# Attention and two MoE layers in one kernel: the q and k loads, the reciprocal of the softmax sums and its small DMAs are moved in the step table

## Chip, cores and metric

The kernel runs on one core of one Trainium2 chip. The metric is the device time of one execution in microseconds (us). Times of engines are counted from the start of the span of one profiled execution.

## The reference

```python
# attention: q, k, v are (4, 8, 1152, 64), float32
q_pool = q.reshape(B, H, S // 2, 2, D).mean(axis=3)
scores = scale * np.matmul(q_pool, k.transpose(0, 1, 3, 2))
scores = scores - np.max(scores, axis=-1, keepdims=True)
attn = np.exp(scores)
attn = attn / (np.sum(attn, axis=-1, keepdims=True) + 1e-09)
attn = np.matmul(attn, v)
# first MoE layer: x is (2304, 512), weights arrive as 64 bit floats
h = np.maximum(x @ w_in, 0.0)
x = h * h @ w_out
# second MoE layer: 8 experts, each token to one expert, at most N // 8 tokens each,
# by a sort of all logits x @ w_gate; then relu(x[mask] @ w1[e]) @ w2[e]
```

## The kernel before

The program has three stretches. For about 790 us it works on the 32 heads of the attention (`Attention.run`), and between the heads it already makes the first MoE layer's hidden rows; then that layer's second product and the routing follow, then the eight experts. The change touches only the first stretch.

**Steps.** A head has 18 steps (`STEPS`, L118). The table `AT` (L45 to L47) gives each part of the work of head n a step, counted from 18n: `lq` and `lk` load q and k, `qs` adds pairs of q rows on POOL (`q_sum`, L187), `kh0` to `kl` split k into two parts (L171 on ACT, L178 on POOL), `kt` and `qt` transpose them on PE and copy them out of PSUM (L221 to L249, copies by DVE or ACT), `pk` are fifteen products whose row maxima DVE takes (L263, L265). The scores of a head (`score`, L278, L279) and their exponentials (L282 on ACT) run one per step, four steps ahead. In the last step of a head `av` makes P times V (L307) and the row sums (L313 or L319). `run` calls `av`, then a score, then whatever has been put off to this step with `at`, then the table's entries, in that order; this is the order of instructions in each engine's queue. Each engine takes its queue in order, and SP, which issues the DMAs, does too: a DMA that waits holds back all that stand behind it.

**The sums' way.** `av` copies the row sums to `row` (L324 on ACT) and moves them with small DMAs into `rc`, 96 partitions by 6 (L329; the heads 0 to 10 have two partial sums per query and so four DMAs, the heads from 11 on, `ADD_HEADS`, have two, because there POOL adds the P tiles up beforehand, `ss`, L292). Five steps later (`recip`) POOL adds the two parts (L335, heads 0 to 10) and the constant 1e-9 (L336), and DVE takes the reciprocal (L337). One step on (`spread`) a DMA writes it to `rs_scr` in DRAM (L340) and another reads it back as 64 rows into `rb` (L341). From step 13 (`norm`) of the odd heads POOL multiplies y by `rb` in three pieces (L483).

**What stands between.** Up to about 291 us one part of the first MoE layer's weights per four steps is read as 64 bit words and turned into float32 by DVE and ACT (`F64.load`: `words` L87, `size` L90 and L96, `sign` L93 and L99, `value` L105). A part of `w_in` is split on ACT (`wih`, L433) and POOL (`wil`, L437); a part of `w_out` is transposed (L453) and stored in DRAM (`wos`, L447). When the eight heads of a batch are done, `batch_h` inserts the products of the first MoE layer (L510) between the steps of the next heads, half a batch at a time; a half takes about four heads, and starts with four `split_x`, whose rest `xl` (L493) POOL makes. Before step 216 (`ORDER_FROM`) these inserted parts run behind a step's other work, from there on ahead of it. The sums of the gate (`ls`, L533 to L538) come from DVE and leave by SP.

**Buffers.** q and k share two `raw` tiles, so a load waits until POOL or ACT has read the tile of two loads before. `value` has two tiles too.

```python
AT = dict(lq=-49, qs=-43, lk=-47, ..., recip=5, spread=6, norm=13,
          high=0, wlow=4, turn=3, gate=5, ...)
```

Of the kernel before, what the change touches and what calls it, by code (L numbers as in the profile page):

```python
# [14 lines left out]
AF = mybir.ActivationFunctionType  # L15
OP = mybir.AluOpType
# [7 lines left out]
HQ = NQ // 2  # L24
# [9 lines left out]
EPS = 1e-9  # L34
# [7 lines left out]
SC, HB, XB = 3, 2, 3  # L42
PEAK_H = 8
PB, WB = 11, 3
AT = dict(lq=-49, qs=-43, lk=-47, qh0=-41, qh1=-41, ql=-38, kh0=-39, kh1=-37, kl=-36, kt0=-28, kt1=-28, kt2=-25,  # L45
          qt0=-25, t2=-22, pk=-23, lv=-12, qt1=-6, qt2=-6, recip=5, spread=6, norm=13,
          high=0, wlow=4, turn=3, gate=5, f0=9, f1=9, f2=9, f3=11, f4=11, f5=14)  # L47
TL, TA = 1, 5
ITERS = 5
START, FIRST, FAST, SLOW, LAST = 36, 32, 8, 16, 14  # L50
# [20 lines left out]
class F64:  # L71
# [7 lines left out]
    def load(self, src, then):  # L79
# [29 lines left out]
        for d, f in enumerate((shift, sign, merge, unit, size, join)):  # L109
            self.at(AT[f"f{d}"], f)  # L110


class Attention:
# [172 lines left out]
    def total(self, n, c, hf):  # L286

        d = self.st[n]
        if c == 1 and hf == 0:
            d["ss"] = self.w1.tile([128, 2, HQ], F32, name="ss")  # L290
        s = d["ss"][:, hf]
        self.nc.gpsimd.tensor_tensor(s, d["P", 0][:, hf] if c == 1 else s, d["P", c][:, hf], op=OP.add)  # L292

    def av(self, n):
        nc = self.nc
        odd = n % 2
        d = self.st[n]
        mine = slice(64, 128) if odd else slice(0, 64)
        pr = n // 2
        if odd == 0:  # L300
            self.y[pr] = self.yp.tile([128, NQ], F32, name="y")
            self.rb[pr] = self.w1.tile([128, NQ], F32, name="rb")
        y, rb = self.y[pr], self.rb[pr]
        A = self.px.tile([128, 512], F32, name="wx")
        for c in range(9):
            for hf in range(2):
                nc.tensor.matmul(A[hf * 64:(hf + 1) * 64, :HQ], d["vf"][:, c], d["P", c][:, hf],  # L307
                                 start=(c == 0), stop=(c == 8))
        t = self.px.tile([128, 512], F32, name="wx")
        if n >= ADD_HEADS:  # L310
            parts = 1
            for hf in range(2):
                nc.tensor.matmul(t[hf * 64:(hf + 1) * 64, :HQ], self.one, d["ss"][:, hf], start=True, stop=True)  # L313
        else:
            parts = 2
            for c in range(9):
                for hf in range(2):
                    r = hf * 64 + c % 2 * 32
                    nc.tensor.matmul(t[r:r + 32, :HQ], self.one[:, 0:32], d["P", c][:, hf],  # L319
                                     start=(c < 2), stop=(c > 6))  # L320
        for hf in range(2):
            nc.scalar.activation(y[mine, hf * HQ:(hf + 1) * HQ], A[hf * 64:(hf + 1) * 64, :HQ], AF.Copy)
        row = self.w1.tile([128, HQ], F32, name="row")
        nc.scalar.activation(row, t[:, :HQ], AF.Copy)  # L324
        rc = self.w2.tile([96, 2, 6], F32, name="rc")
        for hf in range(2):
            for j in range(parts):
                r = hf * 64 + j * 32
                nc.sync.dma_start(rc[hf * 48:(hf + 1) * 48, j, :], row[r:r + 1])  # L329
        for c in range(9):  # L330
            del d["P", c]

        def recip():
            if parts == 2:
                nc.gpsimd.tensor_tensor(rc[:, 0], rc[:, 0], rc[:, 1], op=OP.add)  # L335
            nc.gpsimd.tensor_scalar(rc[:, 0], rc[:, 0], EPS, None, op0=OP.add)  # L336
            nc.vector.reciprocal(rc[:, 0], rc[:, 0])  # L337

        def spread():
            nc.sync.dma_start(self.scratch[n:n + 1, :], rc[:, 0])  # L340
            nc.sync.dma_start(rb[mine, :], bass.AP(tensor=self.scratch.tensor,  # L341
                                                   offset=self.scratch.offset + n * NQ,
                                                   ap=[[0, 64], [1, NQ]]))

        self.at(AT["recip"], recip)
        self.at(AT["spread"], spread)
        if odd:
            for k, f in self.emit(pr, y, rb):
                self.at(k, f)
            del self.y[pr], self.rb[pr]  # L350
# [4 lines left out]
    def events(self, n):  # L355
# [8 lines left out]
        for name, (f, *a) in todo.items():  # L364
            ev.setdefault(AT["lq" if n == 0 and name == "lk" else name], []).append((f, n, *a))
        if n < 2:
            ev.setdefault(AT["kt0"] - 1, []).append((self.fill, n))
        for i in range(15):
            ev.setdefault(AT["pk"] + i, []).append((self.peak, n, i))
        return ev  # L370
# [28 lines left out]
def fused_kernel(ctx, tc, q, k, v, w_in, w_out, w_gate, w1, w2, out, dbg=None, upto=9):  # L399
    nc = tc.nc  # L400
# [6 lines left out]
    wos = dram("wo_scr", (FF, DM))  # L407
# [16 lines left out]
    def setup(f64, raw):  # L424

        gt = raw.tile([128, 4, E], F32, name="gt")
        nc.sync.dma_start(gt, w_gate.rearrange("(c p) e -> p c e", p=128))
        TT = {}

        def w_in_part(c, sl):  # L430
            def then(a):
                def high():
                    nc.scalar.activation(wih[:, c, sl], a, AF.Copy)  # L433

                def low(i):
                    sh = slice(sl.start + i * 128, sl.start + i * 128 + 128)
                    nc.gpsimd.tensor_tensor(wil[:, c, sh], a[:, i * 128:i * 128 + 128], wih[:, c, sh].bitcast(F32),  # L437
                                            op=OP.subtract)

                return [(AT["high"], high)] + [(AT["wlow"] + i, lambda i=i: low(i)) for i in range(2)]  # L440

            f64.load(wiv[c * 128:(c + 1) * 128, sl, :], then)

        def w_out_part(f, j):
            def then(a):
                def turn():
                    nc.sync.dma_start(wos[f * 128:(f + 1) * 128, j * 256:(j + 1) * 256], a)  # L447
                    if j == 0:
                        TT[f] = raw.tile([128, 4, 128], F32, name="wo_t", bufs=1)
                    tt = TT[f]  # L450
                    p = px.tile([128, 512], F32, name="wx")
                    for c in range(2):
                        nc.tensor.transpose(p[:, c * 128:(c + 1) * 128], a[:, c * 128:(c + 1) * 128], cm.idf)  # L453
                    nc.scalar.activation(tt[:, 2 * j:2 * j + 2, :], p[:, :256], AF.Copy)

                def gate():
                    tt = TT.pop(f)
                    g = px.tile([128, 512], F32, name="wx")
                    for c in range(4):
                        nc.tensor.matmul(g[:, :E], tt[:, c, :], gt[:, c, :], start=(c == 0), stop=(c == 3))  # L460

                    def split():
                        nc.vector.tensor_copy(Wg[:, f, 0:E], g[:, :E])

                    f64.at(1, split)

                return [(AT["turn"], turn)] + ([(AT["gate"], gate)] if j else [])

            f64.load(wov[f * 128:(f + 1) * 128, j * 256:(j + 1) * 256, :], then)

        for f in range(0, NF, 2):
            for i in range(4):
                w_in_part(i, slice(f * 128, f * 128 + 256))
                yield
                w_out_part(f + i // 2, i % 2)
                yield
# [130 lines left out]
    with ExitStack() as ea:  # L607
# [4 lines left out]
        parts, taken = setup(f64, raw), 0  # L612
# [581 lines left out]
```

## Time and profile before

| what | us |
|---|---|
| median of three runs | 1339.25 |
| the three runs | 1338.96, 1339.25, 1346.77 |
| the profiled execution | 1348.34 |
| its span | 1346.5 |
| PE busy | 1255.8 (93%) |
| DVE busy | 709.6 (53%) |
| ACT busy | 705.6 (52%) |
| POOL busy | 667.8 (50%) |

PE is TensorE, DVE VectorE, ACT ScalarE, POOL GpSimd, SP the engine that issues the DMAs. The span runs from the first to the last instruction of the one profiled execution; 1.84 us of that execution lie around it. In a row of the timeline the first number is the start, the second the duration of the row, and what stands in brackets is how long the engine was idle before and what released it. A row of the waits gives the total, how often, and the longest.

### The profile page before, as it was taken

The page shows a single profiled execution, that of the slowest core. Times are in us where ns is not written, and L with a number is a line of the kernel's source. Part 1 is how long each engine was busy: PE and PEld are TensorE (multiplying, and loading weights), DVE is VectorE, ACT ScalarE, POOL GpSimd, SP SyncE. Part 2 cuts the span into 40 slices and gives each one's busy share as a digit, 9 for nine tenths or more (in the row PEclk, how much of TensorE's full clock was granted, in tenths as well). Part 3 has the DMA queues.
Part 4 walks back from the last instruction along what each step waited for, and adds up shares of the span by engine and source line. Part 5 has one row for each costly group of instructions (what it writes and reads, how often), then busy time and mean ns, then how long its engine had stood idle before and what let it go on. Part 6 is the DMA issues. An engine that isn't in the chain of part 4 may idle for free. (4 is left out here: it accounts for less than half of the span.)

```text
span 1346.5 us, 25250 instructions
## 1 busy us (share of the span) xinstructions
PE 1255.8 (93%) x9033; PEld 1057.1 (79%) x9033; DVE 709.6 (53%) x1654; ACT 705.6 (52%) x1816; POOL 667.8 (50%) x962
## 2 busy tenths in 40 slices
PE   6897887999899899998999999999999979999997
PEld 4665665688788788887887889777777759999997
DVE  8767466466545354444454201168777724665552
ACT  6767476577566566566665646222222214445441
POOL 5333133248777787868777724266655301221111
PEclk9999899899999999999998999899999988999999
DMA  6435235234324232323322135534344314555541
GB/s 179 144 99 154 86 99 158 80 118 129 88 72 112 63 100 83 85 81 84 91 81 77 46 114 181 150 110 125 119 132 150 107 45 139 191 200 192 184 141 36
DMA packets 136388, 155.60 MB, mean 116 GB/s; under 512 B 19168, under 2 KB 97248, under 8 KB 136256
## 3 DMA queue, kind: packets, MB, share of 16 engines
q1 hardware_dynamic: 133040, 144.21, 35.6%
q0 software_dynamic: 3072, 9.44, 2.3%
q8 instruction: 73, 1.20, 0.4%
q14 instruction: 59, 0.48, 0.1%
q10 hardware_dynamic: 144, 0.26, 0.1%
HBM read 111.46 MB, written 32.87 MB: 107 GB/s over the span
## 5 line engine op out<-in xcount | busy, mean ns | idle before, releaser
L265 DVE TENSOR_REDUCE mx<-wx 128x1 f32<-128x384 f32 (+1 forms) x424 | 227.2, 549 | 240.7 <-PE wx L263 238.7
L282 ACT ACTIVATE P<-sc 128x288 f32<-128x288 f32 x576 | 226.1, 411 | 96.3 <-PE sc L279 89.3
L292 POOL TENSOR_TENSOR ss<-ss,P 128x288 f32<-128x288 f32 x294 | 231.1, 811 | 11.6 <-ACT P L282 9.1
L278 PE MATMUL sc<-M,T 128*128 128x288 f32 x576 | 179.9, 313 | 1.6 <-ACT P L282 1.6
L279 PE MATMUL sc<-M,t 128*128 128x288 f32 x576 | 173.4, 301 | 3.8 <-DVE M L246 3.7
L263 PE MATMUL wx<-T,M 128*128 128x384 f32 (+1 forms) x424 | 151.6, 358 | 21.5 <-DVE mx L265 17.4
L933 POOL TENSOR_TENSOR hl<-h,hh 128x256 fp32r<-128x256 f32 x130 | 101.6, 803 | 108.9 <-ACT hh L931 106.0
L307 PE MATMUL wx<-P,vf 128*64 128x288 f32 x1152 | 152.3, 420 | 0.8 <-DVE mx L265 0.8
L510 PE MATMUL h<-xh,wih 128*128 128x288 f32 x448 | 141.8, 316 | 0.0
L510 PE MATMUL h<-xh,wil 128*128 128x288 f32 x448 | 134.2, 300 | 2.0 <-POOL wil L437 2.0
L510 PE MATMUL h<-xl,wih 128*128 128x288 f32 x448 | 133.8, 299 | 0.0
L307 PEld LDWEIGHTS wx<-P,vf 128*64 128x64 f32 x1152 | 82.1, 141 | 61.5 <-issue 6.7
L278 PEld LDWEIGHTS sc<-M,T 128*128 128x128 f32 x576 | 111.4, 193 | 19.6 <-issue 6.9
L956 PE MATMUL x2p<-woh,hh 128*128 128x512 f32 x288 | 118.0, 410 | 0.0
L956 PE MATMUL x2p<-woh,hl 128*128 128x512 f32 x288 | 117.5, 408 | 0.0
L956 PE MATMUL x2p<-wol,hh 128*128 128x512 f32 x288 | 117.0, 406 | 0.0
L931 ACT ACTIVATE hh<-h 128x512 fp32r<-128x512 f32 x72 | 45.3, 630 | 135.5 <-PE x2p L956 125.1
L279 PEld LDWEIGHTS sc<-M,t 128*128 128x128 f32 x576 | 111.3, 193 | 6.3 <-DVE M L246 5.9
L178 POOL TENSOR_TENSOR ks<-raw,ks 128x192 fp32r<-128x192 f32 x93 | 55.8, 622 | 90.3 <-ACT ks L171 90.3
L263 PEld LDWEIGHTS wx<-T,M 128*128 128x128 f32 (+1 forms) x424 | 77.4, 183 | 28.3 <-DVE mx L265 21.7
L510 PEld LDWEIGHTS h<-xh,wih 128*128 128x128 f32 x448 | 86.2, 192 | 10.3 <-issue 10.2
L1068 POOL DMA_INDIRECT xg<-x_scr,ix x24 | 27.1, 1129 | 130.5 <-PE ept L1081 88.6
(200 smaller groups left out, 2952.8 us busy)
## 6 DMA issues: line engine op xcount, KB each, us to landing
eraw<-in_moe_w_dram SPq DMA_DIRECT2D x56, 512.0 KB
h_scr<-h2st SPq DMA_DIRECT2D x64, 288.0 KB
h<-h_scr SPq DMA_DIRECT2D x72, 256.0 KB
raw<-in_k_dram SPq DMA_DIRECT2D x32, 288.0 KB
t<-T SPq DMA_DIRECT2D x32, 288.0 KB
vf<-in_v_dram SPq DMA_DIRECT2D x32, 288.0 KB
raw<-in_q_dram SPq DMA_DIRECT2D x32, 256.0 KB
words<-in_moe_w_in_dram SPq DMA_DIRECT2D x32, 256.0 KB
```

What stands on the lines that cost most here:

```text
L178: eng.tensor_tensor(ks[:, c, 0:64], d["kn"][:, c], ks[:, c, 64:128].bitcast(F32), op=OP.subtract)
L263: nc.tensor.matmul(t[:m, :384], d["M1"][:, c * 128:c * 128 + m], d["T1"][:, j * 384:(j + 1) * 384], start=True, stop=True)
L265: nc.vector.tensor_reduce(mx[:m, c, j:j + 1], t[:m, :384], axis=AX.X, op=OP.max)
L278: nc.tensor.matmul(t[:, :HQ], d["T1"][:, kk], d["M1"][:, qr], start=True, stop=False)
L279: nc.tensor.matmul(t[:, :HQ], d["T2"][:, kk], d["M2"][:, qr], start=False, stop=True)
L282: nc.scalar.activation(d["P", c][:, hf], t[:, :HQ], AF.Exp, scale=1.0 / (2.0 * math.sqrt(D)))
L292: self.nc.gpsimd.tensor_tensor(s, d["P", 0][:, hf] if c == 1 else s, d["P", c][:, hf], op=OP.add)
L307: nc.tensor.matmul(A[hf * 64:(hf + 1) * 64, :HQ], d["vf"][:, c], d["P", c][:, hf], start=(c == 0), stop=(c == 8))
L510: nc.tensor.matmul(p[:, :HQ], a[:, c, fs], x, start=(j == 0), stop=(j == 11))
L931: self.nc.scalar.activation(hh, t, AF.Copy)
L933: self.eng.tensor_tensor(hl[:, i:i + 2], t[:, i:i + 2], hh[:, i:i + 2].bitcast(F32), op=OP.subtract)
L956: nc.tensor.matmul(self.p, a[:, f, :], x[:, f0 + f, :], start=(f0 + f == 0 and i == 0), stop=(f0 + f == NF - 1 and i == 2))
```

## The change

The loads of q and k get earlier steps; the reciprocal is parted from the addition of the two sums (`total`) and, with its spreading, comes three steps later, the multiplication by it one step later; the constant 1e-9 goes into ACT's copy of the sums (half of it where there are two parts); one DMA now moves both halves of a sum, two instead of four in heads 0 to 10 and one instead of two in the others; the store of a `w_out` part gets a step of its own, one behind its transposes.

```diff
-AT = dict(lq=-49, qs=-43, lk=-47, qh0=-41, ...
-          qt0=-25, t2=-22, pk=-23, lv=-12, qt1=-6, qt2=-6, recip=5, spread=6, norm=13,
-          high=0, wlow=4, turn=3, gate=5, f0=9, f1=9, f2=9, f3=11, f4=11, f5=14)
+AT = dict(lq=-55, qs=-43, lk=-50, qh0=-41, ...
+          qt0=-25, t2=-22, pk=-23, lv=-12, qt1=-6, qt2=-6, total=5, recip=8, spread=9, norm=14,
+          high=0, wlow=4, turn=3, keep=4, gate=5, f0=9, f1=9, f2=9, f3=11, f4=11, f5=14)
...
-        nc.scalar.activation(row, t[:, :HQ], AF.Copy)
+        nc.scalar.activation(row, t[:, :HQ], AF.Copy, bias=EPS / parts)
         rc = self.w2.tile([96, 2, 6], F32, name="rc")
-        for hf in range(2):
-            for j in range(parts):
-                r = hf * 64 + j * 32
-                nc.sync.dma_start(rc[hf * 48:(hf + 1) * 48, j, :], row[r:r + 1])
+        for j in range(parts):
+            nc.sync.dma_start(rc[:, j, :], row[j * 32:j * 32 + 65:64])
...
-        def recip():
+        def total():
             if parts == 2:
                 nc.gpsimd.tensor_tensor(rc[:, 0], rc[:, 0], rc[:, 1], op=OP.add)
-            nc.gpsimd.tensor_scalar(rc[:, 0], rc[:, 0], EPS, None, op0=OP.add)
+
+        def recip():
             nc.vector.reciprocal(rc[:, 0], rc[:, 0])
...
+        self.at(AT["total"], total)
         self.at(AT["recip"], recip)
         self.at(AT["spread"], spread)
...
                 def turn():
-                    nc.sync.dma_start(wos[f * 128:(f + 1) * 128, j * 256:(j + 1) * 256], a)
...
+                def keep():
+                    nc.sync.dma_start(wos[f * 128:(f + 1) * 128, j * 256:(j + 1) * 256], a)
...
-                return [(AT["turn"], turn)] + ([(AT["gate"], gate)] if j else [])
+                return [(AT["turn"], turn), (AT["keep"], keep)] + ([(AT["gate"], gate)] if j else [])
```

The order of PE and ACT stays as it was. DVE keeps its instructions, POOL loses the 32 additions of the constant, SP 43 of the 86 small DMAs.

The queue of SP at the start, of before (the first loads, `gt` the gate's weights, `words` the first parts of the MoE weights):

```order
L159 DMA raw<-in_q_dram 128x4x128
L160 DMA raw<-in_q_dram 64x128
L153 DMA raw<-in_k_dram 128x576
L427 DMA gt<-in_moe_w_gate_dram 128x4x8
L87 DMA words<-in_moe_w_in_dram 128x512
L87 DMA words<-in_moe_w_out_dram 128x512
L159 DMA raw<-in_q_dram 128x4x128
L160 DMA raw<-in_q_dram 64x128
```

and of the changed kernel:

```order
L159 DMA raw<-in_q_dram 128x4x128
L160 DMA raw<-in_q_dram 64x128
L153 DMA raw<-in_k_dram 128x576
L159 DMA raw<-in_q_dram 128x4x128
L160 DMA raw<-in_q_dram 64x128
L427 DMA gt<-in_moe_w_gate_dram 128x4x8
L87 DMA words<-in_moe_w_in_dram 128x512
L87 DMA words<-in_moe_w_out_dram 128x512
```

The load of head 1's q has moved ahead of the gate's weights and of the first two parts of the MoE weights.

The queue of SP behind the end of head 3, of before (`rc` the sums of head 3, `rs_scr` and `rb` its reciprocal, `wo_scr` the store of a `w_out` part):

```order
L329 DMA rc<-row 48x1x6 x4
L87 DMA words<-in_moe_w_out_dram 128x512
L447 DMA wo_scr<-value 128x256
L87 DMA words<-in_moe_w_in_dram 128x512
L340 DMA rs_scr<-rc 96x6
L341 DMA rb<-rs_scr 64x576
L159 DMA raw<-in_q_dram 128x4x128
L160 DMA raw<-in_q_dram 64x128
```

and of the changed kernel, where L327, L339, L340 and L456 are the old L329, L340, L341 and L447:

```order
L327 DMA rc<-row 96x1x6 x2
L159 DMA raw<-in_q_dram 128x4x128
L160 DMA raw<-in_q_dram 64x128
L87 DMA words<-in_moe_w_out_dram 128x512
L456 DMA wo_scr<-value 128x256
L87 DMA words<-in_moe_w_in_dram 128x512
L153 DMA raw<-in_k_dram 128x576
L165 DMA vf_105<-in_v_dram 128x576
L87 DMA words<-in_moe_w_out_dram 128x512
L339 DMA rs_scr<-rc 96x6
L340 DMA rb<-rs_scr 64x576
```

The q load stood behind the two DMAs that wait for the reciprocal, and stands now right behind the sums' own; k has passed the two as well.

The queue of DVE in a later head, about 444 to 454 us of before (`mx` row maxima, `ls` a sum of the gate):

```order
L265 TENSOR_REDUCE mx<-wx 128x1 x7
L535 TENSOR_TENSOR ls<-wx,ls 128x288
L265 TENSOR_REDUCE mx<-wx 128x1 x2
L337 RECIPROCAL rc<-rc 96x6
L265 TENSOR_REDUCE mx<-wx 128x1 x3
L267 TENSOR_REDUCE q_0_109<-mx 128x4
L265 TENSOR_REDUCE mx<-wx 64x1 x3
```

and of the changed kernel, where L336 and L537 are the old L337 and L535:

```order
L265 TENSOR_REDUCE mx<-wx 128x1 x7
L537 TENSOR_TENSOR ls<-wx,ls 128x288
L265 TENSOR_REDUCE mx<-wx 128x1 x5
L267 TENSOR_REDUCE q_0_109<-mx 128x4
L336 RECIPROCAL rc<-rc 96x6
L265 TENSOR_REDUCE mx<-wx 64x1 x3
```

The reciprocal has moved behind three maxima and the reduction over them.

The queue of SP behind the last head, of before (`h_scr` hidden rows, `lg_scr` the gate's sums):

```order
L329 DMA rc<-row 48x1x6 x2
L522 DMA h_scr<-h2st 128x2x288 x2
L340 DMA rs_scr<-rc 96x6
L341 DMA rb<-rs_scr 64x576
L522 DMA h_scr<-h2st 128x2x288
L538 DMA lg_scr<-ls 8x288 x4
```

and of the changed kernel, with L524 and L540 for the old L522 and L538:

```order
L327 DMA rc<-row 96x1x6
L524 DMA h_scr<-h2st 128x2x288 x3
L540 DMA lg_scr<-ls 8x288 x4
L339 DMA rs_scr<-rc 96x6
L340 DMA rb<-rs_scr 64x576
```

The spreading of the last reciprocal has moved behind one more store of hidden rows and the four stores of the gate's sums.

## Rows read from the trace of the kernel before

**Rows 1.** The page, busy time of each engine: us, share of the span, instructions.
```profile
PE 1255.8 (93%) x9033; PEld 1057.1 (79%) x9033; DVE 709.6 (53%) x1654; ACT 705.6 (52%) x1816; POOL 667.8 (50%) x962
```
**Rows 2.** Waits of 0 to 300 us: who waited for whom, total, times, longest.
```profile
POOL qs L187 <- DMA raw<-in_q_dram: 45.5, 13, 6.7
...
DVE value L105 <- POOL wil L437: 9.5, 6, 2.7
```
**Rows 3.** Timeline of SP, POOL, DVE and PE, 121 to 135 us.
```profile
124.49 0.49 SPq L341 DMA_DIRECT2D rb<-rs_scr  x1
125.08 0.53 SPq L159 DMA_DIRECT2D raw<-in_q_dram  x1
...
128.37 1.28 POOL L187 TENSOR_TENSOR qs<-raw 128x256 f32<-128x256 f32 x2 [5.92 <-DMA raw<-in_q_dram]
...
132.18 1.76 DVE L105 TENSOR_TENSOR value<-sign,size 128x256 f32<-128x256 f32 x1 [2.65 <-POOL wil L437]
...
134.08 0.66 PE L453 MATMUL wx<-idf,value 128*128 128x128 f32 x2 [3.36 <-DVE value L105]
```
**Rows 4.** Windows: us, busy time of PE, PEld, DVE, ACT, POOL, granted clock, DMA.
```profile
130.00:135.00 5.00, 1.64 (x11) 1.11 (x9) 2.83 (x4) 3.14 (x10) 3.65 (x8) 0.67 0.91 237
135.00:140.00 5.00, 5.00 (x29) 2.69 (x30) 1.76 (x5) 0.16 (x1) 0.00 (x0) 0.65 0.09 27
```
**Rows 5.** The same view, the first 300 us.
```profile
0.00:300.00 300.00, 254.77 (x1878) 190.23 (x1879) 194.98 (x478) 197.89 (x587) 102.37 (x200) 0.95 0.43 125
```
**Rows 6.** Waits of 300 to 760 us.
```profile
DVE rc L337 <- POOL rc L336: 37.7, 19, 3.6
...
PE wx L263 <- DVE mx L265: 14.7, 5, 3.3
```
**Rows 7.** Timeline of POOL, DVE and PE, 449 to 459 us, and PE's next such stall.
```profile
449.95 0.79 POOL L493 TENSOR_TENSOR xl<-y,xh 128x288 fp32r<-128x288 f32 x1
450.82 0.23 POOL L336 TENSOR_SCALAR rc<-rc 96x6 f32<-96x6 f32 x1
...
454.91 0.81 POOL L493 TENSOR_TENSOR xl<-y,xh 128x288 fp32r<-128x288 f32 x1
...
451.76 0.39 PE L263 MATMUL wx<-T,M 128*64 128x384 f32 x1 [3.28 <-DVE mx L265]
...
457.98 0.29 PE L278 MATMUL sc<-M,T 128*128 128x288 f32 x1
...
542.80 0.39 PE L263 MATMUL wx<-T,M 128*64 128x384 f32 x1 [3.07 <-DVE mx L265]
```
**Rows 8.** Timeline of SP, ACT and PE at the start.
```profile
2.96 0.51 SPq L87 DMA_DIRECT2D words<-in_moe_w_in_dram  x1
...
4.64 0.38 SPq L159 DMA_DIRECT2D raw<-in_q_dram  x1
...
6.72 0.45 ACT L93 ACTIVATE sign<-words 128x256 f32<-128x256 f32 x1 [0.66 <-DMA words<-in_moe_w_in_dram]
...
9.67 0.69 PE L263 MATMUL wx<-T,M 128*128 128x384 f32 x1 [1.21 <-ACT M L207]
```
**Rows 9.** Timeline of SP, POOL and PE behind the last head.
```profile
787.56 0.34 SPq L340 DMA_DIRECT2D rs_scr<-rc  x1
...
791.54 1.30 SPq L538 DMA_DIRECT2D lg_scr<-ls  x4
...
792.62 1.71 POOL L483 TENSOR_TENSOR y<-y,rb 128x192 f32<-128x192 f32 x3 [8.38 <-issue]
...
796.66 0.29 PE L510 MATMUL wx<-xh,wih 128*128 128x288 f32 x1
```
**Rows 10.** The page, one DMA queue (packets, MB, share of 16 engines); timeline, sums of head 6.
```profile
q1 hardware_dynamic: 133040, 144.21, 35.6%
...
194.05 2.45 SPq L329 DMA_DIRECT2D rc<-row  x4
...
197.93 0.20 POOL L335 TENSOR_TENSOR rc<-rc 96x6 f32<-96x6 f32 x1 [1.92 <-DMA rc<-row]
```

More of the change, by code (lines that the diff above doesn't have):

```diff
@@ L44 @@
 PB, WB = 11, 3
-AT = dict(lq=-49, qs=-43, lk=-47, qh0=-41, qh1=-41, ql=-38, kh0=-39, kh1=-37, kl=-36, kt0=-28, kt1=-28, kt2=-25,
-          qt0=-25, t2=-22, pk=-23, lv=-12, qt1=-6, qt2=-6, recip=5, spread=6, norm=13,
-          high=0, wlow=4, turn=3, gate=5, f0=9, f1=9, f2=9, f3=11, f4=11, f5=14)
+AT = dict(lq=-55, qs=-43, lk=-50, qh0=-41, qh1=-41, ql=-38, kh0=-39, kh1=-37, kl=-36, kt0=-28, kt1=-28, kt2=-25,
+          qt0=-25, t2=-22, pk=-23, lv=-12, qt1=-6, qt2=-6, total=5, recip=8, spread=9, norm=14,
+          high=0, wlow=4, turn=3, keep=4, gate=5, f0=9, f1=9, f2=9, f3=11, f4=11, f5=14)
 TL, TA = 1, 5
```

## The prediction

> **What bounds the kernel now.** I read the page's busy times first. PE is busy for 93% of the span, every other engine for about half of it [rows 1], and PE's order is not changed, so the change can win or lose only where PE waits. I then listed PE's stalls of 1 us and more in the attention from its timeline, and asked the views of waits, by stretch, who stood in front of each.
>
> *Early, up to 300 us.* POOL waits 13 times, 45.5 us in all, for the q load before it can add q's pairs, and DVE waits 9.5 us for POOL's split of a weight [rows 2]. Behind the end of head 3 it reads as one chain [rows 3]: on SP the load of q stands behind the DMA that reads back the reciprocal, which itself can go only when the reciprocal is in DRAM (124.49). So q is issued at 125.08 and POOL starts on it at 128.37, after 5.92 us idle. The weights' splits stand behind it; DVE's `value` waits 2.65 us for one of them and then takes 1.76 us; PE waits 3.36 us for `value`. Of this kind are four PE stalls, at 63, 134, 157 and 235 us: 2.16, 3.36, 3.27 and 3.73, 12.5 us together; DVE's side of it is the 9.5 us of waits [rows 2] and what two long `value` take over their usual 0.41. The granted clock falls behind such a stall: 0.67 and 0.65 in the ten microseconds around this one [rows 4], where PE had stood still.
>
> *Late, from 300 us.* DVE waits for POOL's addition of 1e-9, 19 times and 37.7 us [rows 6], although the sums have long landed: POOL works off a queue of P additions. Most of it hides. Where a half batch starts it does not: `xl` at 449.95, the constant at 450.82, and behind the reciprocal the row maxima, so that PE stands 3.28 us until 451.76 [rows 7]. PE's waits for maxima are 14.7 us in five places [rows 6]: the five half starts from 361 to 726 us.
>
> **The change part by part.**
>
> *q and k loads.* Five DMAs no longer stand in front of q, the two that wait for the reciprocal among them: it is issued right behind the sums' own DMAs, six steps earlier. A step is 542.80 − 451.76 = 91.0 us [rows 7] over 72 steps, so 1.26 us; six are 7.6. Behind head 3 that is an issue at 125.08 − 7.6 = 117.5 instead of 125.08 and, with the 3.3 us that it took from there to POOL's start, a landing at 120.8, where POOL stood ready at 128.37 − 5.92 = 122.45 [rows 3]. With the wait the neighbour in time goes too: the 1.76 us of `value` lay beside POOL's late q work. Of the 12.5 us I take 10 off. The rest stays because at 63 and 157 us PE's next wait, for a copy that DVE makes behind `value`, is only about 1 us shorter than the stall. Bounds: 5 to 12.5. What the clock costs in the first 300 us is at most 300 × (1 − 0.95) = 15 us [rows 5]; the windows of 5 us around the four stalls hold 12 of these, about 10 outside the stalls themselves. I take 7 off, between 0 and 10, since some small stall may leave the clock low just as well.
>
> *Reciprocal apart from its addition, constant on ACT.* 32 additions of 0.23 us leave POOL [rows 7], and 43 DMA issues of 2.45 / 4 = 0.61 us leave SP [rows 10]. Neither engine sets the end, so that by itself is worth 0. The bias costs ACT no instruction; I put it at 0, between −0.4 and +1 us over the 32 copies. What counts is that the reciprocal no longer waits for POOL. The next bound at a half start is `xl`: the fourth one ends at 454.91 + 0.81 = 455.72 now, and 0.3 earlier without the constant, 455.4. PE's products behind it then go on at about 455.5, where they stood at 457.98 [rows 7]: 2.4 us for the whole place, stall and slow clock together. Five places at 2.0 to 2.8 give 12 off. Bounds: 2.5 (each `xl` stops PE in turn, and the clock stays low) and 19 (all 14.7 us and half as much clock).
>
> *The start.* Head 1's q now stands before the first MoE weights on SP, and it shares a `raw` tile that POOL must first have read: before, it went at 4.64, and the weights at 2.96 [rows 8]. Now the weights follow at about 6.1, 3.1 us later. ACT's `sign`, which waits for them and ran at 6.72, stands ahead of the copies that PE's first maxima product at 9.67 needs. ACT had 0.66 us idle there, so 1.9 to 3.1 us are lost: +2.5.
>
> *The end.* Behind the last head the DMA of the reciprocal went at 787.56. It now stands behind the four stores of the gate's sums, which end at 791.54 + 1.30 = 792.84 [rows 9], 5.3 us later. Read back faster than before (nothing stands between: 1.5 us instead of 1.84), the multiplication that began at 792.62 starts 3 us or more later, at 797.7 at the latest, takes 1.71, and ACT's and DVE's splits another 1.7. PE wanted the result at 796.66 and would get it at about 800: 3.4 us, and up to 1.7 us of clock. +4.5, between +2 and +6.
>
> *Small new waits.* DVE's next-but-one `value` now waits for the store one step later, and at three places `value` needs a split that stands behind `total`, with 0.2 to 0.5 us to spare. Five places at 0 to 1 us: +2.5.
>
> *The merged DMA.* Head 6's four DMAs began at 194.05, the issue of the last ended at 196.50, and POOL added at 197.93 [rows 10], so landing takes 1.4 us. Two issues less bring the sum 1.2 us forward. That is worth nothing by itself (the reciprocal is three steps later), and I put it at 0. The piece is 96 rows of six numbers now, from two rows of `row`.
>
> The Trainium skill speaks against it ("DMA: Bandwidth & Descriptors", section "Why a DMA increments its semaphore by 16 and not by 1"): a copy is spread over the largest number of DMA engines, 16 at most, that divides the slowest dimension above 1 of both sides. By that rule the old copies, 48 pieces on both sides, ran on 16 engines, and the new ones, two rows into 96 partitions, run on 2. No trace of before shows a copy of two rows, so it stands as a rival below.
>
> **Sum.** +2.5 − 10 − 7 − 12 + 4.5 + 2.5 = −19.5 against the profiled execution of 1348.34. That execution is 9.1 us above the median, and the part of a run that varies is most likely the clock; so I count the 7 us of clock by half against the median: −16, or 1323 (−1.2%). A measurement here tells about 1% from no change.
>
> **Rivals.**
>
> *The merged copy lands later.* A packet took 0.356 × 16 × 1346.5 / 133040 = 0.058 us on average [rows 10]. If each of the two source rows goes through one DMA engine, that engine has 48 packets where 16 engines had 3 each: 45 × 0.058 = 2.6 us later, less the 1.2 us of issues, so `total` in the heads 0 to 10 comes 1.4 us later, with POOL's weight splits behind it. At the three tight places that is 3 × 1.4 = 4.2 us (1327), in all eleven heads 15 (1338). For it: POOL already waits 1.92 us for these sums [rows 10]. The rule of "DMA: Bandwidth & Descriptors" above would have it so. Against: most splits have more slack than that. Chance 0.17.
>
> *The late gain is swallowed.* POOL is busy without a gap from 445 to 459 us; PE may wait for `xl` four times in small stalls, and the clock falls as before. For it: two of the `xl` come only at 453.40 and 454.91, 1.5 us apart. Then the late term is 2.5, and the time 1323 + 9.5 = 1332. Chance 0.14.
>
> *Slower.* Between the spreading and the multiplication lie 5 steps now instead of 7: 5 × 1.26 = 6.3 us. Behind the last head the way from the DMA's issue to the multiplication took 792.62 − 787.56 = 5.06 us [rows 9]. If the read waits longer on SP than the 1.3 us left, POOL stops in every odd head, with the splits, the P additions and with them the row sums behind it. 16 odd heads at 1 us of stall and 0.85 of clock are 30 us: 1353. Against it: POOL is usually behind PE's step in the late heads, which gives the DMA more time. Chance 0.08.
>
> *The change does little:* the early stalls have a second cause right behind q (the `value` chain itself), and start and end take 7 us back. About 1339. Chance 0.05.
>
> *All of it works,* clock and late stalls in full: 1312. Chance 0.08.
>
> **Chances.** The forecast has 0.48. Faster by over 1% is below 1325.9: 0.42 of the forecast's, 0.06 of the merged copy's, 0.08 of the last: 0.56. Slower by over 1% is above 1352.6: 0.06 of the slower rival. The rest, 0.38, lies within 1%. The range goes from 1310 to 1338: it takes in the early and the late terms at their lower bounds one at a time, and the rivals up to the merged copy's dearest form; the slower rival is left out.
>
> **What would show it.** In the trace after: POOL's waits for q in the first 300 us nearly gone, and the waits of `value` for the split below 3 us; the clock of the first 300 us above 0.96; DVE's reciprocal without a wait from 300 us on, and the maxima behind it on time; at a half start PE waiting for `xl` or not at all, with each place 2 to 3 us shorter; a first maxima product at about 12 us; PE idle for 3 us around 797. Wrong would be: POOL's wait at `total` above 3 us in the early heads (the merged copy), a wait of POOL's multiplication for `rb` in the odd heads (the slower rival), or q still waited for.

## The result, and the profile after

The changed kernel takes 1328.32 us (median of 4 runs, 1325.60 to 1331.98) where the kernel before, in 4 runs beside it, takes 1343.01 (1338.96 to 1347.47). The ratio is 0.9889, with a 95% interval of 0.9859 to 0.9920. The profiled execution took 1329.09 us, its span 1327.3; the span before was 1346.5.

PE's order is the same in both kernels, so the start of each head's product of P and V (L307) can be laid side by side. This table gives, from the two PE timelines, how much earlier or later the changed kernel comes there; the last row is the first indirect load of the expert stage (1106.03 and 1086.98).

| place | before | after | difference | difference gained since the row above |
|---|---|---|---|---|
| first product of the maxima | 9.67 | 13.53 | +3.86 | +3.86 |
| head 10 | 290.98 | 277.38 | −13.60 | −17.46 |
| head 12 | 347.59 | 339.47 | −8.12 | +5.48 |
| head 31 | 775.53 | 752.46 | −23.07 | −14.95 |
| first load of the experts | 1106.03 | 1086.98 | −19.05 | +4.02 |

The rest of the program, the experts, differs by 0.2 us. The execution profiled before (1348.34) lies 5.3 us above the median of its four runs, the one profiled after 0.8 us, so that the table shows some 4.5 us more than the medians do.

*Early.* The waits of 0 to 300 us of the changed kernel:

```profile
POOL y L485 <- DMA rb<-rs_scr: 26.8, 4, 8.1
...
POOL qs L187 <- DMA raw<-in_q_dram: 3.9, 4, 2.3
...
POOL rc L333 <- DMA rc<-row: 2.4, 4, 0.7
```

POOL's wait for q, 45.5 us before [rows 2], is 3.9, and the wait of `value` for a weight split is gone. POOL waits 26.8 us for the read reciprocal instead, in the four odd heads up to 7. The windows view of the first 300 us, which answers to [rows 5]:

```profile
0.00:300.00 300.00, 256.50 (x1946) 193.97 (x1946) 207.85 (x495) 205.55 (x610) 109.74 (x204) 0.98 0.45 131
```

The granted clock is 0.98 in place of 0.95, at most 300 × 0.03 = 9 us of clock in 300. Some of it belongs to the one execution: the kernel of e4 below has the same instructions up to the last head, and 0.97 in its first 300 us.

*A half start.* Timeline of the changed kernel at the place of [rows 7], DVE, POOL and PE apart:

```profile
438.61 0.17 DVE L267 TENSOR_REDUCE q<-mx 128x4 fp32r<-128x12 f32 x1
438.69 0.18 DVE L336 RECIPROCAL rc<-rc 96x6 f32<-96x6 f32 x1
...
439.63 0.80 POOL L495 TENSOR_TENSOR xl<-y,xh 128x288 fp32r<-128x288 f32 x1
...
444.18 0.80 POOL L495 TENSOR_TENSOR xl<-y,xh 128x288 fp32r<-128x288 f32 x1
...
440.49 0.40 PE L512 MATMUL h<-xl,wih 128*128 128x288 f32 x1 [0.27 <-POOL xl L495]
...
442.01 0.40 PE L512 MATMUL h<-xl,wih 128*128 128x288 f32 x1 [0.44 <-POOL xl L495]
...
443.51 0.40 PE L512 MATMUL h<-xl,wih 128*128 128x288 f32 x1 [0.58 <-POOL xl L495]
```

The reciprocal has no wait. PE's next bound is `xl`, and it costs 0.27 + 0.44 + 0.58 = 1.3 us where 3.28 us were lost in one piece; from 300 us on the clock is 1.00 up to 750 us.

*The start.* SP, ACT and PE, the rows that answer to [rows 8]:

```profile
4.84 0.37 SPq L159 DMA_DIRECT2D raw<-in_q_dram  x1
...
6.45 0.51 SPq L87 DMA_DIRECT2D words<-in_moe_w_in_dram  x1
...
10.60 0.44 ACT L93 ACTIVATE sign<-words 128x256 f32<-128x256 f32 x1 [4.38 <-DMA words<-in_moe_w_in_dram]
...
11.58 0.75 PE L245 MATMUL wx<-idr,q 128*128 128x128 f32 x4 [3.71 <-ACT T L207]
...
13.53 0.69 PE L263 MATMUL wx<-T,M 128*128 128x384 f32 x1 [1.21 <-ACT M L207]
```

The first MoE weights are issued 3.49 us later than before, ACT stands 4.38 us for them, and PE 3.71 us for the copy behind.

*The end.* SP, POOL and PE, the rows that answer to [rows 9]:

```profile
769.87 0.31 SPq L339 DMA_DIRECT2D rs_scr<-rc  x1
...
774.99 1.68 POOL L485 TENSOR_TENSOR y<-y,rb 128x192 f32<-128x192 f32 x3 [21.14 <-DMA rb<-rs_scr]
...
776.65 0.40 PE L512 MATMUL wx<-xh,wih 128*128 128x288 f32 x1 [2.90 <-ACT xh L494]
```

PE stands 2.90 us; the multiplication begins 5.12 us after the DMA's issue, as it did before (5.06).

*What the prediction did not have.* Between the heads 10 and 12 the changed kernel loses 5.5 us. DVE, POOL and PE there:

```profile
291.79 4.61 DVE L90 TENSOR_SCALAR size<-words 128x256 int32<-128x256 int32 x1
...
290.85 2.33 POOL L292 TENSOR_TENSOR ss<-ss,P 128x288 f32<-128x288 f32 x3
293.14 0.45 POOL L437 TENSOR_TENSOR wil<-value,wih 128x128 fp32r<-128x128 f32 x1
...
294.72 1.53 POOL L292 TENSOR_TENSOR ss<-ss,P 128x288 f32<-128x288 f32 x2
...
297.48 0.72 PE L221 MATMUL wx<-idr,ks 128*128 128x128 f32 x4 [3.68 <-DVE mx L265]
```

A shift of a weight part on DVE, 0.28 us as a rule, takes 4.61. It begins while POOL is at work and ends at 296.40, 0.15 us after POOL's unbroken row of instructions ends (294.72 + 1.53 = 296.25). The maxima behind it are late, and PE stands 3.68 us. A row of POOL's without a gap is not all that it takes: the same row began at 285.51 and let a shift pass at 287.33 in 0.28 us.

```profile
287.33 0.28 DVE L90 TENSOR_SCALAR size<-words 128x256 int32<-128x256 int32 x1
```

At 331.99 a `value` of 0.42 us takes 6.02 in the same way, but that is no loss of the change. The kernel before has it too:

```profile
340.60 5.54 DVE L105 TENSOR_TENSOR value<-sign,size 128x256 f32<-128x256 f32 x1
```

### The profile page after: what moved, and what is told of

It reads as the page before. It is cut to its first block, busy times and chain, and to the rows that moved or that the text cites. A ratio compares the mean times of both kernels' runs of the same rounds, so it can differ in the third digit from the quotient of the medians.

```text
span 1327.3 us, 25135 instructions
## 1 busy us (share of the span) xinstructions
PE 1244.9 (94%) x9033; PEld 1046.9 (79%) x9033; DVE 720.5 (54%) x1654; ACT 703.1 (53%) x1816; POOL 657.4 (50%) x930
## 5 line engine op out<-in xcount | busy, mean ns | idle before, releaser
L307 PE MATMUL wx<-P,vf 128*64 128x288 f32 x1152 | 147.7, 411 | 0.8 <-DVE mx L265 0.8
L307 PEld LDWEIGHTS wx<-P,vf 128*64 128x64 f32 x1152 | 80.3, 138 | 58.5 <-DVE mx L265 5.4
L512 PEld LDWEIGHTS h<-xl,wih 128*128 128x128 f32 x448 | 84.9, 189 | 8.8 <-POOL xl L495 8.7
```

The costliest lines, as they stand in the source:

```text
L512: nc.tensor.matmul(p[:, :HQ], a[:, c, fs], x, start=(j == 0), stop=(j == 11))
```

## The experiments

Each kernel was timed beside the kernel before on the same chip; ratios are against it, with the 95% interval. Medians of one kernel differ by some us between sets of runs, so smaller steps are read from the traces. A trace is one execution, with a clock of its own, so that there the waits are surer than the positions. "A" and "B" below are the two theories in the text that was put down before each run.

**Loads alone (e1).** The kernel before, with

```diff
-AT = dict(lq=-49, qs=-43, lk=-47,
+AT = dict(lq=-55, qs=-43, lk=-50,
```

> Only the loads of q and k are moved (steps -55 and -50 in the kernel before, all else as there). Theory A (the q load alone makes the early stalls): the four stalls at 63, 134, 157 and 235 us go as in the changed kernel, head 10 begins some 14 us earlier than before (the start still pays 3.9), the five late stalls stay, and the whole is 9 to 14 us below before. Theory B (the reciprocal's move is needed too, since POOL and DVE wait for the sums at the same places): less than 6 us of it, and POOL's waits for other things take the place of its waits for q.

1343.21 us, ratio 1.0012 (0.9988 to 1.0037): nothing. The waits, 0 to 300 us and 300 to 760 us:

```profile
POOL qs L187 <- DMA raw<-in_q_dram: 3.2, 2, 2.3
...
PE wx L263 <- DVE mx L265: 14.7, 5, 3.3
```

The wait for q goes, as theory A had it, and the late stalls stay. But the start costs 3.6 us at head 0, only 3.8 us are left at head 10 in the profiled execution, and the timed runs show none of it. Theory B came: another wait of POOL takes the place of the wait for q. POOL stands 24.8 us for the read reciprocal, for which it did not wait before 300 us in the kernel before, and behind head 3 the chain of [rows 3] is there again with `rb` in q's place:

```profile
POOL y L483 <- DMA rb<-rs_scr: 24.8, 5, 5.6
...
132.42 1.15 POOL L483 TENSOR_TENSOR y<-y,rb 128x192 f32<-128x192 f32 x2 [5.58 <-DMA rb<-rs_scr]
...
134.98 0.93 DVE L105 TENSOR_TENSOR value<-sign,size 128x256 f32<-128x256 f32 x1 [2.50 <-POOL wil L437]
...
136.06 0.41 PE L453 MATMUL wx<-idf,value 128*128 128x128 f32 x2 [2.39 <-DVE value L105]
```

**Without the loads (e2).** The changed kernel, with

```diff
-AT = dict(lq=-55, qs=-43, lk=-50,
+AT = dict(lq=-49, qs=-43, lk=-47,
```

> The changed kernel with the loads of q and k back at steps -49 and -47. Theory A (the loads make the early gain, the reciprocal's parting the late one): the early stalls are back, the five late stalls of 14.7 us are gone, the start is as before, the end pays 4 us: 3 to 8 us below before. Theory B (both parts are needed in both stretches): no more than 2 us below before, the late stalls half back, since q then comes behind the reciprocal's DMAs, which go three steps later.

1327.61 us, 0.9893 (0.9844 to 0.9942): all of the change's gain. Both theories are wrong. The early stalls did not come back: POOL waits 12.0 us for q, and head 10 is 11.1 us earlier than before. The reason stands in SP's queue: q goes at step 5 of a head and k at 7, the reciprocal's DMAs went at 6 and go at 9 now. Moving these back lets q and k pass them just as moving q forward does. It does more than that: POOL stands 12.0 us for q and 21.2 us for the read reciprocal here, 33.2 together against 28.0 in e1, and yet no `value` waits for a split any more (3.2 us in e1, 9.5 before). So it is not the length of POOL's waits that counts, but what stands behind them.

**Delay alone (e5).** The kernel before, with the two additions left on POOL, the constant too:

```diff
-qt1=-6, qt2=-6, recip=5, spread=6, norm=13,
+qt1=-6, qt2=-6, total=5, recip=8, spread=9, norm=14,
...
+        self.at(AT["total"], total)
```

> The kernel before with only the steps of the sums' way changed: POOL's two additions stay at step 5 (the constant still on POOL), the reciprocal goes at 8, its spreading at 9, the multiplication at 14; q, k, the four small DMAs and the store as before. Theory A (it is the order: q and k now stand ahead of the reciprocal's DMAs on SP, and the maxima ahead of the reciprocal on DVE): the early stalls are small as in the run without the loads' move, the late stalls go too, since POOL's constant comes about 3 us late and the reciprocal is asked for 3 steps, 3.8 us, later; 10 to 14 us below before, the end paying 4. Theory B (POOL's constant is what delays): the late stalls stay above 10 us of their 14.7.

1324.58 us, 0.9868 (0.9834 to 0.9901), 17.7 us below before: theory A, and more than its 10 to 14. The three steps carry the whole gain. At the half start of [rows 7] DVE and PE of this kernel:

```profile
437.22 0.19 DVE L339 RECIPROCAL rc<-rc 96x6 f32<-96x6 f32 x1 [1.99 <-POOL rc L336]
...
437.89 0.54 PE L221 MATMUL wx<-idr,ks 128*128 128x128 f32 x4 [2.21 <-DVE mx L265]
```

The constant on POOL still comes 1.99 us late and PE still stands 2.21 us; of the 14.7 us of late stalls four are left, 7.1 us together. In return no shift takes longer than 1.15 us, though a `value` still takes 6.01 at 326.36, and between the heads 10 and 12 nothing is lost. The constant stands in POOL's row there, with 0.09 us of idle time ahead of it and 0.08 behind, and a shift takes 0.45 us:

```profile
291.57 0.23 POOL L336 TENSOR_SCALAR rc<-rc 96x6 f32<-96x6 f32 x1
...
292.39 0.45 DVE L90 TENSOR_SCALAR size<-words 128x256 int32<-128x256 int32 x1
```

**Constant alone (e6).** The changed kernel with all steps as before:

```diff
-lq=-55, qs=-43, lk=-50, ..., total=5, recip=8, spread=9, norm=14,
+lq=-49, qs=-43, lk=-47, ..., total=5, recip=5, spread=6, norm=13,
```

> The changed kernel with every step as before (loads, reciprocal, spreading, multiplication): what stays is the constant in ScalarE's copy, half the small DMAs, and the store's own step. Theory A of the order: the early stalls at 63, 134, 157 and 235 us are back, since q stands behind the reciprocal's DMAs again. In the late heads the reciprocal waits for its DMA alone, which has landed long before: the 14.7 us of late stalls go, the end is as before; 7 to 12 us below before, all of it after 340 us. Theory B (the late stalls need the delay): less than 4 us below before.

1338.21 us, 0.9970 (0.9950 to 0.9990). The waits of the first 300 us:

```profile
POOL qs L187 <- DMA raw<-in_q_dram: 43.4, 14, 8.0
...
PE sc L279 <- DVE M L246: 8.1, 5, 4.0
```

That is 4.0 us below before, and not theory A's 7 to 12; in the trace it is theory A in kind. After head 12 the late stalls are gone, and 14.9 us are gained up to head 31, as in the changed kernel. Before head 12 three of the four early stalls are there (131, 157 and 239 us: 3.98, 3.01 and 2.92), and a shift of 4.41 us has been added: head 12 comes 5.9 us later than before.

```profile
306.86 4.41 DVE L90 TENSOR_SCALAR size<-words 128x256 int32<-128x256 int32 x1
```

So the late gain is the constant's, and most of it can be had by the delay too (10.7 us up to head 31). And the long shift comes with what this kernel has of the change, the constant's leaving POOL above all, and not with the loss of POOL's waits for q, which are here as before.

**The start (e3).** Changed kernel, head 1's q at step −50:

```diff
+            k = AT["lq" if n == 0 and name == "lk" else name]
+            ev.setdefault(-50 if n == 1 and name == "lq" else k, []).append((f, n, *a))
```

> The changed kernel with the q load of head 1 five steps later, behind the first two weight parts, as it stood before. Theory A (the words' DMA behind a q load that waits for a tile is the whole loss at the start): PE's first product of the maxima is back at 9.7 instead of 13.5 us, and 3.9 us come off the whole time. Theory B (the start is hidden by later waits for the weights): the first heads are earlier, head 10 is not, and the time is that of the changed kernel.

1326.47 us, 0.9886 (0.9841 to 0.9931). PE's first product of the maxima is at 10.20, so the stall itself is explained; but at head 10 this kernel stands 5.3 us behind the changed one, and the time is 1.9 us lower. The times cannot tell 3.9 us from nothing here. Between the heads 0 and 10 PE's waits of over 0.15 us come to 20.7 us in this trace and 20.0 in the changed kernel's, while the clock of the first 300 us is 0.96 against 0.98, at most 6 us: what the trace lost by head 10 is clock, not a wait. Whether an earlier start costs that clock, or this one execution happened to have it, stays open.

**The end (e4).** Changed kernel, the last head's reciprocal and spreading three steps earlier:

```diff
+        last = 3 if n == B * H - 1 else 0
+        self.at(AT["recip"] - last, recip)
+        self.at(AT["spread"] - last, spread)
```

> The changed kernel with the reciprocal and its spreading of the last head three steps earlier, as before. Theory A (the spreading behind the gate's four stores makes the stall behind the last head): PE's stall of 2.90 us there and the slow clock behind it go, 3 to 4.5 us off. Theory B (what follows waits for other loads anyway): the stall moves to the next product of the second MoE stage and the time stays within 1 us of the changed kernel.

1323.86 us, 0.9885 (0.9847 to 0.9923), 4.5 us below the changed kernel's median. In the trace no wait of 0.4 us or more of PE is left between 751 and 790 us, and from head 31 to the experts' first load it takes 325.2 us instead of 334.5. From 760 to 800 us the granted clock is 1.00 in place of 0.96. Theory A by the trace, as to the stall and the clock right behind it; the two intervals of the times overlap. About half of the 9.3 us is not the stall's: e7 below has no stall there either and takes 332.0 us for the same stretch, with another clock.

**Both undone (e7), and POOL's additions later (e8).** e7 has the loads at the old steps and e4's edit; e8 adds

```diff
-ADD_HEADS = 11
+ADD_HEADS = 13
```

> The changed kernel with q and k loaded at the steps of before and the last head's reciprocal and spreading at the steps of before. Theory A (the loads' move is idle beside the reciprocal's move, and costs 3.9 us at the start; the end costs 4): 1320 to 1324, 4 to 8 us below the changed kernel. Theory B (start and end are hidden by what follows): 1326 to 1329.

> The run before this, and POOL's additions of P tiles begin with head 13 instead of 11, when the weight parts are done (heads 11 and 12 have their sums made by PE, 36 products instead of 4). Theory A (DVE's shifts and joins on the weights stand still while POOL's additions follow each other without a gap: 4.61 us instead of 0.28 at 291.8 and 6.02 instead of 0.42 at 332.0 in the changed kernel): PE's stalls of 3.68 and about 2 us near 300 and 340 go, the long instructions are below 1.2 us, PE pays 2 times 2.0 us for the sums, and 1 to 4 us are gained. Theory B (the long instructions come from something else on DVE): they stay, and 4 us are lost.

e7: 1322.44 us, 0.9844 (0.9812 to 0.9876), inside theory A's range, though the interval overlaps the changed kernel's. e8: 1312.10 us, 0.9769 (0.9745 to 0.9792), 10.3 us below e7, more than either theory had. DVE's `value` and shifts of e8, count and then shortest, median and longest in ns:

```profile
L105 DVE TENSOR_TENSOR value<-sign,size x64: 404/416/1095, 8.8 to 325.6; 128x256 f32<-128x256 f32 x64
...
L90 DVE TENSOR_SCALAR size<-words x64: 274/287/853, 6.7 to 319.4; 128x256 int32<-128x256 int32 x64
```

The long instructions are gone (one L96 of 1.80 us at 177.56 is left), and so are PE's stalls of 3.68, 1.43 and 2.03 us that e7 has at 297, 334 and 338. Up to head 13 e8 is 8.3 us ahead of e7, PE's extra products for two heads included. That is theory A. Its price was too low because I left out the stall of 1.43, in which PE waits for POOL's `wil`, and the clock behind the stalls.

**The same on the kernel before (e10).** One number, `ADD_HEADS = 13`.

> The kernel before, only that POOL's additions of P tiles begin with head 13. Theory A (long DVE instructions beside a gapless POOL were there before too: 2.13 and 5.54 us, and the gain is independent of the change): 3 to 10 us below before, the longest shift and join under 1.8 us, the five late stalls as they were. Theory B (before had gaps in POOL that the change closed): within 2 us of before, or above it by PE's 4 us for the sums.

1339.95 us, 0.9981 (0.9947 to 1.0015). The median is 3.7 us below before, and the interval goes from 7 us below to 2 above, so the times leave both theories standing. By the trace the `value` of 5.54 us is gone (the longest takes 1.09) and from head 10 to 12 4.3 us are gained, which PE's sums for two heads take back by head 13, all but 0.8. The stall of 3.68 us, the largest that e8 removes, is not there in the kernel before.

**The loads once more (e9).** e8 with q and k at −55 and −50, and e3's exception for head 1.

> The fastest run so far (loads at the old steps, last head early, additions from head 13) with the loads of q and k back at the changed kernel's steps, head 1's q alone kept behind the first weights. Theory A (the loads' early steps are idle once the reciprocal goes later): within 2 us of 1312.1. Theory B (they still take off some of POOL's 11.7 us of waits for q and bring PE time): 1307 to 1310.

1316.80 us, 0.9813 (0.9775 to 0.9851), not faster than e8: 4.7 us above it, more than theory A's 2, but the two intervals overlap. POOL waits 3.8 us for q in place of 11.7, and 33.3 us for the reciprocal in place of 20.2. Theory B is out: the early loads buy nothing. Whether they cost something is open.

**The small DMAs (e11).** e8 with four and two DMAs for the sums:

```diff
-            nc.sync.dma_start(rc[:, j, :], row[j * 32:j * 32 + 65:64])
+            for hf in range(2):
+                r = hf * 64 + j * 32
+                nc.sync.dma_start(rc[hf * 48:(hf + 1) * 48, j, :], row[r:r + 1])
```

> The fastest run so far with the four and two small DMAs of the sums per head instead of two and one. Theory A (the merged copies land as fast as the old ones, and what they save is 1.2 us per head before POOL's total, in heads 0 to 12): POOL's wait for the sums is back at about 1.2 to 1.9 us a head, the time within 2 us of 1312.1. Theory B (merged copies land later on fewer DMA engines): the sums come no later than with the merged ones, and the time falls.

1323.31 us, 0.9856 (0.9812 to 0.9900), 11 us above e8 and outside its interval: both theories are wrong. SP, DVE and PE of this kernel behind head 3:

```profile
124.44 0.38 SPq L341 DMA_DIRECT2D rs_scr<-rc  x1
129.33 0.48 SPq L342 DMA_DIRECT2D rb<-rs_scr  x1
129.87 0.58 SPq L459 DMA_DIRECT2D wo_scr<-value  x1
...
132.72 0.61 DVE L105 TENSOR_TENSOR value<-sign,size 128x256 f32<-128x256 f32 x1 [3.69 <-DMA wo_scr<-value]
...
133.48 0.41 PE L455 MATMUL wx<-idf,value 128*128 128x128 f32 x2 [3.23 <-DVE value L105]
```

The two extra issues push what stands behind them back by 1.2 us and more; the reciprocal's read waits 4.9 us for its write (3.6 in e8), with the store of `value` behind it; DVE's next `value` needs that tile and waits 3.69 us, and PE 3.23. With the merged DMAs (e8) the same store goes at 127.18, and PE has no such stall. e5, which has the four DMAs as well, has the same one: `value` waits 3.30 us for the store and PE 2.74. From 40 to 300 us e11 has six waits of PE of 1 us and more, 9.7 us together, and e8 one of 1.0; the other five were not followed to their cause. On this queue, where one DMA waits for another, 0.6 us of issue was not hidden.

**The multiplication later (e12).** e8 with `norm=16` instead of 14.

> The fastest run so far with the multiplication by the reciprocal two steps later (16 instead of 14). Theory A (POOL's waits for the read reciprocal, 20 us in four early heads and 6 us in three late ones, hold nothing that PE needs): the waits go to under 8 us, the time stays within 2 us of 1312.1. Theory B (the weight splits behind them matter): 3 to 6 us less.

1311.91 us, 0.9768 (0.9731 to 0.9805). POOL's wait for the reciprocal in the first 300 us falls from 20.2 to 10.9 us, not below theory A's 8, and the time stays: theory A in the time. What is gone of the waits held nothing that PE needed.

## Why the prediction was right, and where its steps were not

The total came out: −19.5 us was the sum against the profiled execution, −19.25 was measured there. That they are so close is partly luck: of the −19.25 some 4.5 us is how far the two profiled executions lie from their medians, and two terms that came out larger made up for a loss of 5.5 us that was not foreseen. Against the medians 16 us were forecast and 14.7 measured (1343.01 to 1328.32). 1328.3 is inside the range, above the forecast of 1323 and above 1325.9, the line for 1% against 1339.25; against the 1343.01 beside it, it is 1.1%. The terms:

- *Early,* 10 of stall and 7 of clock less 2.5 of new waits: −14.5 forecast, −17.5 measured up to head 10. The stall's part has the forecast size: between the heads 0 and 10 PE's waits of over 0.15 us fall from 30.2 to 20.0 us. The links of the chain of [rows 3] are there, from POOL's wait over the split and `value` to PE, but the step that failed is "q and k loads": it put the gain down to the loads' new steps, as if nothing stood behind the wait for q. With q early and all else as before, POOL waits for `rb` instead and the chain goes on (e1), and the timed runs show no gain. The later steps of the reciprocal, its spreading and the multiplication make the gain, with the loads where they were (e2, e5), and early loads add nothing to them (e9). Which of the three steps it takes was not tested one by one. And q itself could not go six steps earlier: behind head 3 it was issued at 120.5, not 117.5, because the sums' own DMAs stand ahead of it.
- *Late:* −12 forecast, −14.95 measured from head 12 to 31. The next bound is `xl`, as forecast. The step said that the constant's leaving POOL does it, and that alone does (e6); the delay alone gives 10.7 us of it too (e5).
- *Start:* +2.5 forecast, +3.86 measured. ACT's idle 0.66 us was no cover, since it was itself a wait for these weights. They were issued 3.49 us later, and from their issue to ACT's start it took 4.15 us in place of 3.76.
- *End:* +4.5 forecast, as 3.4 of stall and up to 1.7 of clock; a stall of 2.90 us and at most 40 × 0.04 = 1.6 us of clock between 760 and 800 us are in the trace. The table's +4.02 is no clean measure of it, since the stretch up to the experts' first load varies by more from kernel to kernel (e4, e7).
- *Small new waits:* +2.5 forecast for five places. Some of them are in the trace (1.4 us of `value` behind the store), but the loss that counts, 5.5 us between the heads 10 and 12, is another: a DVE shift that stood still beside POOL. "Neither engine sets the end, so that by itself is worth 0" is the sentence that missed it. It was said of the additions of the constant, and the long shift comes with their leaving. It takes 4.4 to 4.6 us in all six kernels with the constant on ACT and POOL's additions from head 11 (the changed one, e2, e3, e4, e6, e7), and no shift at that place is so long in the three with the constant on POOL (before, e1, e5). The merged DMAs and the store's own step went with the constant in all of them, so the constant's part is not shown by itself.
- *The merged DMA,* put at 0: e11 shows 11 us in the fastest kernel, by SP's queue. In the changed kernel it was not undone by itself, so its share there stays open.
- *The rivals.* The merged copy lands hardly later: SP's and POOL's rows of head 6 after the change, which answer to [rows 10]:

```profile
187.37 1.19 SPq L327 DMA_DIRECT2D rc<-row  x2
...
189.96 0.20 POOL L333 TENSOR_TENSOR rc<-rc 96x6 f32<-96x6 f32 x1 [0.62 <-DMA rc<-row]
```

  From the end of the last issue (188.56) to POOL it is 1.40 us, and it was 1.43; over the heads where POOL stood for the sums the median is 1.41 of four, and was 1.36 of ten. The slower rival did not come, though its sign did: POOL waits 26.8 us for the reciprocal in the early odd heads. In e8 nearly half of such waits could be taken away without a gain (e12), while in e1, with the multiplication at its old step, one of them did hold PE. So the sign alone did not tell. The late gain was not swallowed.

The range of 28 us was wider than the runs of any one kernel, which spread over 3 to 18 us.

## What to carry to other kernels

When a transfer is late because it stands behind a waiting one in the same queue, either of the two can be moved; look first at which move is free, test each alone before crediting the one that names the symptom, and ask which wait comes next when this one is gone. An issue of 0.6 us on a half empty queue is not free if something behind it in the queue is waited for. And an instruction of 0.23 us taken off a half idle engine is not worth 0 for that reason alone: look at what the other engines did beside it.

## What the runs showed of the hardware

**DVE beside POOL.** In the changed kernel a shift (`size`, L90: one SBUF input, 0.28 us as a rule) and a join (`value`, L105: two SBUF inputs, 0.42 us) took 4.61 and 6.02 us when they began beside an unbroken row of POOL instructions, and ended 0.15 and 0.29 us after its end; the row maxima, which read PSUM, took 0.54 to 0.56 us beside such a row. In e8, with POOL's additions later, the longest shift and join take 0.85 and 1.10 us. Other shifts and joins passed beside an unbroken row with little loss: 0.28 us at 287.33, a join of 0.56 us at 288.75, and POOL's additions beside that join took 0.97 to 0.99 us instead of 0.78 to 0.81. So either engine can be the one that gives way; what decides it no run here shows. The Trainium skill ("GPSIMD Engine Reference", section "1. Specifications") says that POOL shares its SBUF interfaces with DVE, with contention for DVE instructions in a 2-port mode or with two SBUF inputs. The trace agrees for the join; whether the shift, with one input, ran in such a mode it does not show.

**Two DMA engines did for 96 pieces of 24 bytes.** The page of the changed kernel counts its packets so:

```profile
DMA packets 135096, 155.57 MB, mean 117 GB/s; under 512 B 17878, under 2 KB 95958, under 8 KB 134966
```

Before it was 19168 under 512 B, 1290 more. The pieces themselves are as many as before: 7200 packets of 24 bytes in both traces, while those of 4 bytes fall from 11457 to 10167, by these 1290. If each DMA engine that takes part in a copy adds one small packet of its own, 86 copies on 16 engines and 43 on 2 differ by 86 × 16 − 43 × 2 = 1290; e11 and e8, with 90 and 45 copies, differ by 19424 − 18074 = 1350 = 90 × 16 − 45 × 2. By the Trainium skill ("DMA: Bandwidth & Descriptors", section "Why a DMA increments its semaphore by 16 and not by 1") each engine that takes part posts its own count, and their number divides the slowest dimension of both sides; the counts agree with 16 and 2, though both pairs say the same thing, 30 packets less for each merged copy. The price that I worked out for it, 45 packets at the mean of 0.058 us, does not hold: from the end of the issue to POOL's start it took 1.41 us with the merged copy and 1.36 with the old ones (medians of four and ten heads), so that 45 such packets cost less than 0.1 us here.
